# Four seven-product units in the third token tile, and the VectorE sums that have to be ready for them

## The chip, the cores and the metric

The kernel runs on one core of a Trainium2 chip. The metric is the device time of one launch in microseconds (us). The kernel before takes 278.38 us, the median of 3 runs (278.06 to 278.6). Its profiled execution took 278.12 us, of which the trace covers a span of 276.4 us; all times inside the trace are counted from the start of that span. The granted TensorE clock was 0.999 of full speed over the run.

## What is computed

Two stages, one after the other. The first is an attention over pooled keys and values, the second a gated feed-forward product over its output:

```python
# q, k, v: 8 batches, 8 heads, 576 positions, 64 values per head
k_p, v_p = k and v averaged over groups of 8 positions      # 72 pooled positions
attn = softmax(q @ k_p^T / sqrt(64))
x = (attn @ v_p), heads side by side                        # 4608 tokens x 512
h = x @ w_in                                                # 4608 x 2048
g = h * sigmoid(h)
out = g @ w_out                                             # 4608 x 512, float32
```

## The kernel before

The 4608 tokens are worked off in nine **tiles** `t = 0..8` of 512 tokens. In each tile TensorE does an "up" product (`x @ w_in`, transposed so that `h_T` has the 2048 hidden values on 16 groups `g` of 128 partitions), ScalarE applies SiLU, TensorE does a "down" product (`h @ w_out`), and in between it computes the attention of the batch that later tiles need.

Most of the large products use **seven products of quarter blocks in place of eight**. Seven products numbered 1 to 7 take sums or differences of blocks on both sides, and VectorE and ScalarE combine the results. In the up product such a **unit** covers four of the sixteen groups; the units are called A, B, C and E here and in the kernel's token strings, so `C5` is product 5 of unit C. The weight sums of a unit never change and are made once; the sums of x (`x_sum`) are made anew for each tile:

```python
    UNITS = ((4, 6), (8, 10), (12, 14), (0, 2))      # A, B, C, E: groups of two
    U_W = {2: ((1, 0), (1, 1)), 5: ((0, 0), (0, 1)), 1: ((0, 0), (1, 1)),
           6: ((1, 0), (0, 0)), 7: ((0, 1), (1, 1))}  # five weight sums for each unit
    ...
    def unit_weight_sum(y, n):                        # L442, 128x512 bf16 on VectorE
        nc.vector.tensor_tensor(out=w_sum1[y][U_WI[n]], in0=UW[y][a], in1=UW[y][b], op=...)
    def unit_x_sum(t, n):                             # L449, 128x512 bf16 on VectorE
        nc.vector.tensor_tensor(out=x_sum[:, U_XI[n]], in0=x_quarter(t, *a), in1=x_quarter(t, *b), op=...)
    def unit_x(t, n):
        if n in U_XI:
            return x_sum[:, U_XI[n]]
        return x_quarter(t, 0, 0) if n == 2 else x_quarter(t, 1, 1)   # products 2 and 5: x itself
    ...
        def stage(y, n):          # bank P takes products 2, 4, 7; Q takes 5, 3, 6; R takes 1
            if n == "2":
                product(y, 2, "P", True)
                nc.scalar.copy(r_sb, ps[y, "P"])
            elif n == "5":
                product(y, 5, "Q", True)
                tt(out=rr_sb, in0=ps[y, "Q"], in1=r_sb, op=ALU.add)       # L514
            elif n == "1":
                product(y, 1, "R", True)
                tt(out=t_sb, in0=ps[y, "R"], in1=rr_sb, op=ALU.subtract)  # L517
            elif n == "3":
                product(y, 3, "Q", False)     # adds to bank Q, so rr_sb must have been read
                hidden(y, 0, 1, ps[y, "Q"])
            ...                               # 4, 7, 6: L526, L529 and the SiLU of the results
```

One product of a unit is four matmuls of 256 columns. A group that is not in a unit is a plain product: four matmuls of 512 columns (`plain`, L547).

Three recipes exist, chosen by the tile:

- **t = 0**: plain products up and down.
- **t = 1 and 2**: `up` with an item list (two units and eight plain groups in t = 1; three units A, B, C and the plain groups 0 to 3 in t = 2), then `down_quarters`, the down product in seven products that begins with products 2 and 5. VectorE's and other work is placed by step: a list entry `(step, function)` is recorded once that many steps of TensorE's work have been recorded.
- **t = 3 to 8** (`t >= T4`): `run(t)`, one fixed token string with four units, whose down product (`down_stages`) begins with product 4, on plain h, and has its products interleaved with the up product's end.

```python
    PROGRAM = (
        "C2 C5 B2 B5 q0 C4 C1 C3 q3 B4 C7 B3 B1 Ca C6 A2 Cs B7 A5 B6 E2 A4 Ba E5 A1 Bs "
        "A3 h7h A7 E4 E3 q1 E1 A6 Aa k As E7 q2 E6 d40 d41 d42 Ea h5h d43 h2h d30 Es "
        ...
        "d52 d53 d10 sc2 de1 h6h d11 h7l u2 d12 d13 d70 nu0 nu1 de2 d71 T2 d72 d73 d60 "
        "x3 d61 d62 x7 x6 d63 o x4 x1 "
    )
```

In `run`, the tokens `u1` and `u2` are two subtractions on GpSimd (L754), behind the loads of the next batch in GpSimd's program. The part of `down_quarters` that ends a tile t = 1 or 2, with the work that is recorded among it:

```python
            product(3, 0, KQ, cc)
            nc.vector.tensor_copy(out=o_sb[0][:, cs, HI], in_=ps["Q"][:, cs])               # L682
            product(7, 0, KQ, cc)
            tt(out=o_sb[0][:, cs, LO], in0=ps["P"][:, cs], in1=t_sb[:, cs], op=add)         # L686
            ...
            product(6, 0, KQ, cc)
            tt(out=o_sb[1][:, cs, HI], in0=ps["Q"][:, cs], in1=t_sb[:, cs], op=add)         # L690
    ...
        # attention of batch a: the last part of xT that the next tile needs
        tensor_mul(out=xT[...], in0=nu[c], in1=rec)                                         # L398
        # sums of x for the next tile
            for n in (4, 1, 3, 7, 6):
                f_down.append((98 if t < B - 1 else 44, lambda n=n: unit_x_sum(t + 1, n)))
        if t == 1:
            ...
            f_down.append((72, unit_weight_tiles))
            for i, n in enumerate(U_W):
                f_down.append((73 if i < 2 else 81, lambda n=n: unit_weight_sum(2, n)))
        if t == 2:
            for i, n in enumerate(U_W):
                f_down.append((76 + 2 * i, lambda n=n: unit_weight_sum(3, n)))
```

Besides these, `hidden_sum(n, k0, k1)` (L615) makes the sums of h for the down product, half of the groups at a time (`h2` lower half, `h1` upper half and so on), and `weight_sum(n, i)` (L633) makes quarters of the down product's weight sums.

Of the kernel before, what the change touches and what calls it, by code (L numbers as in the profile page):

```python
# [36 lines left out]
def kernel(  # L37
# [11 lines left out]
    B, H, S, D = q.shape  # L49
# [90 lines left out]
    def load_q(b, halves=False):  # L140
        st = batches.setdefault(b, {})
        q_bf = mid.tile([128, 2, QI * D], BF16, tag="q_bf", name="q_bf")
        if halves:
            pass
        elif b == B - 1:

            for s in range(4):
                for a in range(2):
                    nc.gpsimd.dma_start(
                        out=q_bf[QP * s : QP * (s + 1), a, :].rearrange(  # L150
                            "p (i d) -> p i d", d=D
                        ),
                        in_=q[b, 4 * a + s].rearrange("(i p) d -> p i d", p=QP),
                    )
        else:
            nc.gpsimd.dma_start(out=q_bf, in_=q_r[b])
        st["q_bf"] = q_bf
        st["qT"] = mid.tile([128, 2, QI, QP, 2], BF16, tag="qT", bufs=1, name="qT")
# [41 lines left out]
    def behind_x_sums(n=6):  # L200
        nc.gpsimd.tensor_copy(out=gate[:1], in_=x_sum[:1, U_XI[n], 0, :1])

    def pool_k(b):
        pool_rows(kp[:SP], batches[b]["k_raw"])
# [114 lines left out]
    def part(g, f):  # L319
        return ((g, f * QF, (f + 1) * QF),)  # L320
# [3 lines left out]
    def third(n):  # L324
        return tuple((g, n * QV, (n + 1) * QV) for g in range(2))
# [31 lines left out]
    def denominators(b, segs, on_dve=False):  # L357
        st = batches[b]
        w = width(segs)
        es = st["es", segs]  # L360
        den_ps = ps_tile([128, 512], FP32, "at", "den_ps")
        for s in range(4):
            nc.tensor.matmul(  # L363
                den_ps[32 * s : 32 * (s + 1), :w],
                lhsT=ones, rhs=es[:, s, :], start=True, stop=True,
            )
        rec = mid.tile([128, VW], FP32, tag="rec", bufs=3, name="rec")[:, :w]
        if on_dve:
            nc.vector.reciprocal(rec, den_ps[:, :w])
        else:  # L370
            lnd = mid.tile([128, VW], FP32, tag="lnd", bufs=1, name="lnd")[:, :w]
            nc.scalar.activation(lnd, den_ps[:, :w], func=AF.Ln)  # L372
            nc.scalar.activation(rec, lnd, func=AF.Exp, scale=-1.0)
        st["rec", segs] = rec

    def numerators(b, segs, tags=("at", "at")):
        st = batches[b]
        w = width(segs)
        g0, i0, i1 = segs[0]
        c0 = b * S % NX + i0 * QP  # L380
        cols = slice(c0, c0 + (i1 - i0) * QP)
        es = st.pop(("es", segs))
        rec = st.pop(("rec", segs))
        nu = []
        for c in range(2):
            nu_ps = ps_tile([128, 512], FP32, tags[c], "nu_ps")
            for g, _, _, cs in seg_cols(segs):
                for s in range(4):
                    nc.tensor.matmul(  # L389
                        nu_ps[32 * s : 32 * (s + 1), cs],  # L390
                        lhsT=st["vp"][:, 4 * g + s, c::2],
                        rhs=es[:, s, cs],
                        start=True, stop=True,
                    )
            nu.append(nu_ps)
        ng = len(segs)
        for c in range(2):
            nc.vector.tensor_mul(  # L398
                out=xT[:, 2 * g0 + c : 2 * (g0 + ng - 1) + c + 1 : 2, cols],
                in0=nu[c][:, :w].rearrange("r (g n) -> r g n", g=ng),  # L400
                in1=rec.rearrange("r (g n) -> r g n", g=ng),
            )
# [8 lines left out]
    def spread(fillers, n):  # L411
# [5 lines left out]
        for f in todo:  # L417
# [11 lines left out]
    U_W = {2: ((1, 0), (1, 1)), 5: ((0, 0), (0, 1)), 1: ((0, 0), (1, 1)),  # L429
           6: ((1, 0), (0, 0)), 7: ((0, 1), (1, 1))}  # L430
# [9 lines left out]
    def unit_weight_sum(y, n):  # L440
        a, b = U_W[n]
        nc.vector.tensor_tensor(  # L442
            out=w_sum1[y][U_WI[n]], in0=UW[y][a], in1=UW[y][b],
            op=ALU.subtract if n in (6, 7) else ALU.add,
        )

    def unit_x_sum(t, n):
        a, b = U_X[n]
        nc.vector.tensor_tensor(  # L449
            out=x_sum[:, U_XI[n]], in0=x_quarter(t, *a), in1=x_quarter(t, *b),  # L450
            op=ALU.subtract if n in (3, 4) else ALU.add,
        )
# [148 lines left out]
    def quarter(i, j, ks):  # L601
        return h_T[:, j * KQ + ks.start : j * KQ + ks.stop, i * NQ : (i + 1) * NQ]
# [9 lines left out]
    def hidden_sum(n, k0, k1):  # L612
        a, b, op = H_SUMS[n]
        ks = slice(k0, k1)
        nc.vector.tensor_tensor(  # L615
            out=h_sum[n][:, ks, :], in0=quarter(*a, ks), in1=quarter(*b, ks), op=op
        )
# [10 lines left out]
    PW = 4  # L628
# [156 lines left out]
    def run(t):  # L785
# [13 lines left out]
        if a == B - 1:  # L799
            toks.insert(1 + max(toks.index("de2"), toks.index("nu1"), toks.index("o")), "nu2")  # L800
        if t == T4:
            toks.insert(0, "T2")
        if attn:
            if a + 1 < B - 1:
                load_q(a + 1)
            behind_x_sums(6 if t == T4 else gate_on)
            pool_k(a)
# [131 lines left out]
    def load_half_2(name, half):  # L939
        for i0, i1 in ((0, SA), (SA, SLOTS), (SLOTS, SLOTS + 1)):  # L940
            load_slots(nc.gpsimd, 2, name, i0, i1, half)

    THREE = (
        "A2 A5 g0 B2 A4 A1 A3 B5 C2 A7 B4 A6 Ah B1 B3 As C5 B7 C4 B6 Bh C1 C3 C7 Bs g1"
        " C6 Ch Cs g2 g3",
        "A2 A5 g0 A4 B2 A3 A1 B5 A7 C2 A6 B4 B3 B1 C5 Ah B7 As C4 Bh B6 C1 C3 C7 Bs g1"
        " C6 Ch Cs g2 g3",
    )
    visits = [third(n) for n in range(3)]
    T4 = 3  # L950
    for t in range(NT):
        a = t + 1
        if t >= T4:
            run(t)
            continue
        f_up, f_down = [], []
        if t == 0:
            GA = 11
            items = [(g, 0, HS) for g in range(GA)]
            items += [(g, HS, NTT - HS) for g in range(GA)]  # L960
            items += [(g, 0, NTT) for g in range(GA, KG)]
            f_up += [(1, lambda: denominators(0, part(0, 1), on_dve=True))]
            f_up += [(5, lambda: denominators(0, part(1, 1), on_dve=True))]
            f_up += [(13, lambda: numerators(0, part(0, 1)))]
            f_up += [(17, lambda: numerators(0, part(1, 1)))]
        else:
            G = lambda *gs: [(g, 0, NTT) for g in gs]
            if t == 1:
                items = (
                    G(12, 13, 14, 15) + [(0, "25143"), (1, "2"), (0, "7"), (1, "5")]  # L970
                    + [(0, "6h"), (1, "1")] + G(0) + [(1, "4"), (0, "s"), (1, "3")] + G(1)
                    + [(1, "7h6")] + G(2) + [(1, "s")] + G(3)
                )
            else:
                items = []
                for it in THREE[t // B].split():
                    items += [(("BCA".index(it[0])), it[1])] if it[0] in "ABC" else G(int(it[1]))
            if t == 1:
                for n in U_X:
                    f_up.append((0, lambda n=n: unit_x_sum(t, n)))  # L980
            for n in (2, 5):
                h_at = 50 if t == B else 54 if t > 1 else 45
                f_up.append((h_at, lambda n=n: hidden_sum(n, 4, 8)))
            f_up.append((56, lambda: hidden_sum(6, 4, 8)))
            for n, k0 in ((2, 0), (5, 0), (1, 4), (1, 0)):
                f_up.append((64, lambda n=n, k0=k0: hidden_sum(n, k0, k0 + 4)))
            f_down.append((33 if t > 1 else 44, lambda: hidden_sum(7, 0, 8)))
            f_down.append((71 if t < B else 50, lambda: hidden_sum(6, 0, 4)))

        for n, t0, f_to, at, parts in (  # L990
            (1, 0, f_down, 16, (0, 2)), (3, 0, f_down, 30, (0, 2)),
            (1, 0, f_down, 46, (2, PW)), (3, 0, f_down, 50, (2, PW)),
            (6, 0, f_down, 8, (0, PW)), (4, 0, f_down, 12, (0, 2)),
            (7, 0, f_down, 14, (0, 2)), (4, 1, f_down, 20, (2, PW)), (7, 1, f_down, 52, (2, PW)),
        ):
            for i in range(*parts):
                if t == t0:
                    f_to.append((at + i, lambda n=n, i=i: weight_sum(n, i)))
# [63 lines left out]
        if t == 1:  # L1062
# [6 lines left out]
            f_down.append((72, unit_weight_tiles))  # L1069
            for i, n in enumerate(U_W):  # L1070
                f_down.append((73 if i < 2 else 81, lambda n=n: unit_weight_sum(2, n)))
        if t == 2:
            for i, n in enumerate(U_W):
                f_down.append((76 + 2 * i, lambda n=n: unit_weight_sum(3, n)))
        if t != 1:
            moe_tables()
        if t == 0:
# [34 lines left out]
```

The softmax here doesn't subtract the row's maximum and nothing guards it: scores larger than these inputs give would overflow.

## Time and profile before

| | |
|---|---|
| time | 278.38 us (278.06 to 278.6) |
| span of the trace | 276.4 us |
| TensorE busy | 271.7 us, 98% |
| VectorE busy | 243.9 us, 88% |
| ScalarE busy | 192.4 us, 70% |
| GpSimd busy | 111.6 us, 40% |
| tile t = 1, down part | 64.69 to 80.88 us |
| tile t = 2 | 80.88 to 109.61 us |
| tile t = 3 | 109.61 to 137.95 us |

The tile boundaries are the starts of the first matmul of each part in the timeline of TensorE. In the timelines each row is a run of like instructions of one engine: start in us, time in us from the first's start to the last's end, engine, source line, operation, output tile and input tiles, shapes, count, and in brackets the idle time before the row and what ended it. The share of busy time is an average; to learn what a change in one tile is worth, one has to look at who waits for whom in that tile, and the start-to-start distances of the matmuls show best whether TensorE went on without a pause.

### The profile page before, as it was taken

The numbers are of one execution on the slowest core, as the hardware profiler recorded it, in microseconds if no ns is written. First come the engines' busy times: TensorE is split into PE (matmuls) and PEld (weight loads), VectorE is DVE, ScalarE is ACT, GpSimd is POOL, SyncE is SP. The second block draws the span as 40 slices with busy tenths as digits, with TensorE's granted clock in tenths as the row PEclk, the third lists the DMA queues.
The fourth block names the chain that finished last, engine by engine and source line by source line (L and its number), as shares of the span: only waits on it lengthen the run. The fifth ranks groups of instructions, "written<-read, shape, count | busy, mean of one in ns | idle before, by whom it ended". The sixth has DMA issues, their size and how long they took to land.

```text
span 276.4 us, 7372 instructions
## 1 busy us (share of the span) xinstructions
PE 271.7 (98%) x2933; PEld 209.7 (76%) x2933; DVE 243.9 (88%) x452; ACT 192.4 (70%) x374; POOL 111.6 (40%) x112
## 2 busy tenths in 40 slices
PE   8999999999999999999999999999999999999995
PEld 4448444576778678887888778877887788888884
DVE  4986778778998879998999999999999899998994
ACT  1688767468668976789777986798688868407730
POOL 8755116252148530964377426976450400000000
PEclk9999999999999999999999999999999999999999
DMA  7999999986849879468746844599620032005003
GB/s 214 276 245 252 207 306 196 257 161 118 165 56 216 228 106 180 119 180 127 129 115 176 144 72 126 135 155 128 131 66 2 2 100 55 0 12 145 1 26 129
DMA packets 31314, 37.73 MB, mean 137 GB/s; under 512 B 10352, under 2 KB 22256, under 8 KB 31280
## 3 DMA queue, kind: packets, MB, share of 16 engines
q0 software_dynamic: 23920, 27.03, 52.7%
q1 hardware_dynamic: 6928, 9.58, 12.5%
q10 hardware_dynamic: 432, 0.66, 0.6%
q8 instruction: 23, 0.38, 0.6%
q14 instruction: 11, 0.09, 0.1%
HBM read 36.70 MB, written 9.44 MB: 167 GB/s over the span
## 4 chain that ended last, share of the span: by engine, by line
PE 83%; DMA 14%; issue 1%; POOL 0%; DVE 0%; POOLq 0%
PE u_psP L493 14%; PE u_psQ L493 14%; PE o_psQ L712 12%; PE o_psP L712 12%; DMA w_in_sb<-in_moe_w_in_dram 6%; DMA w_out_sb<-in_moe_w_out_dram 6%; PE u_psR L493 5%; PE o_psR L712 4%; PE o_psQ L656 4%; PE o_psP L656 4%; PE hp_ps L547 4%; PE sc_ps L345 3%; PE nu_ps L389 3%; PE o_ps L582 2%; DMA q_bf<-in_q_dram 2%; PE den_ps L363 2%
## 5 line engine op out<-in xcount | busy, mean ns | idle before, releaser
L615 DVE TENSOR_TENSOR h_sum<-h_T 128x1024 bf16<-128x1024 bf16 (+1 forms) x78 | 59.2, 803 | 2.8 <-ACT h_T L501 1.6
L493 PEld LDWEIGHTS <-w_sum 128*128 128x128 bf16 x532 | 52.0, 98 | 7.2 <-issue 0.3
L712 PEld LDWEIGHTS <-h_sum 128*128 128x128 bf16 x480 | 45.8, 98 | 8.1 <-issue 2.5
L353 ACT ACTIVATE es<-sc_ps 72x384 bf16<-72x384 f32 (+1 forms) x100 | 39.1, 471 | 5.4 <-PE sc_ps L345 5.3
L501 ACT ACTIVATE h_T<-c_sb 128x512 bf16<-128x512 f32 x58 | 35.7, 630 | 6.2 <-DVE c_sb L529 3.6
L511 ACT COPY r_sb<-u_psP 128x512 f32<-128x512 f32 x29 | 17.0, 586 | 19.2 <-PE u_psP L493 19.2
L547 PE MATMUL hp_ps<-xT,w_in_sb 128*128 128x512 bf16 (+2 forms) x156 | 26.6, 319 | 0.0
L398 DVE TENSOR_TENSOR xT<-nu_ps,rec 128x384 bf16<-128x384 f32 (+1 forms) x50 | 23.9, 529 | 1.7 <-PE nu_ps L389 1.4
L493 PEld LDWEIGHTS <-w_in_sb 128*128 128x128 bf16 x232 | 22.5, 98 | 3.2 <-DVE x_sum L449 0.3
L195 POOL TENSOR_TENSOR raw<-raw 72x1024 f32<-72x1024 f32 x10 | 23.6, 2365 | 0.1
L514 DVE TENSOR_TENSOR rr_sb<-u_psQ,r_sb 128x512 f32<-128x512 f32 x29 | 19.5, 684 | 3.6 <-PE u_psQ L493 1.9
L559 POOL DMA_DIRECT2D out_dram<-o_sb x2 | 1.2, 617 | 52.2 <-ACT o_sb L726 48.1
L553 ACT ACTIVATE h_T<-hp_ps 128x512 bf16<-128x512 f32 (+2 forms) x39 | 18.1, 477 | 5.9 <-PE hp_ps L547 5.1
L526 DVE TENSOR_TENSOR c_sb<-u_psP,t_sb 128x512 f32<-128x512 f32 x29 | 19.8, 682 | 1.9 <-PE u_psP L493 1.3
L547 PEld LDWEIGHTS <-w_in_sb 128*128 128x128 bf16 x156 | 14.6, 98 | 8.5 <-issue 0.8
L517 DVE TENSOR_TENSOR t_sb<-u_psR,rr_sb 128x512 f32<-128x512 f32 x29 | 19.6, 676 | 1.5 <-PE u_psR L493 0.5
L754 POOL TENSOR_TENSOR rr_sb<-rr_sb,o_sb 128x512 f32<-128x512 f32 x8 | 14.3, 1782 | 15.9 <-ACT o_sb L726 12.6
L529 DVE TENSOR_TENSOR c_sb<-u_psQ,t_sb 128x512 f32<-128x512 f32 x29 | 19.6, 677 | 1.0 <-PE u_psQ L493 0.8
L712 PEld LDWEIGHTS <-h_T 128*128 128x128 bf16 x192 | 18.5, 98 | 2.7
L501 ACT ACTIVATE h_T<-u_psP 128x512 bf16<-128x512 f32 x29 | 17.3, 598 | 3.5 <-PE u_psP L493 3.5
L501 ACT ACTIVATE h_T<-u_psQ 128x512 bf16<-128x512 f32 x29 | 17.3, 596 | 3.4 <-PE u_psQ L493 3.4
L372 ACT ACTIVATE lnd<-den_ps 128x384 f32<-128x384 f32 (+1 forms) x23 | 11.2, 487 | 11.3 <-PE den_ps L363 11.3
(106 smaller groups left out, 585.4 us busy)
## 6 DMA issues: line engine op xcount, KB each, us to landing
out_dram<-o_sb SPq DMA_DIRECT2D x128, 64.0 KB, 1.8
raw<-in_k_dram POOLq DMA_DIRECT2D x10, 576.0 KB, 7.9
raw<-in_v_dram POOLq DMA_DIRECT2D x10, 576.0 KB, 7.7
q_bf<-in_q_dram POOLq DMA_DIRECT2D x6, 576.0 KB, 10.6
w_in_sb<-in_moe_w_in_dram POOLq DMA_DIRECT2D x8, 256.0 KB, 8.3
w_out_sb<-in_moe_w_out_dram POOLq DMA_DIRECT2D x4, 512.0 KB, 13.5
raw<-in_v_dram POOLq DMA_DIRECT2D x2, 768.0 KB, 11.1
raw<-in_k_dram POOLq DMA_DIRECT2D x1, 768.0 KB, 10.7
```

Source lines behind the costliest of these rows:

```text
L195: nc.gpsimd.tensor_add(out=raw[:, :, : 2 * D], in0=raw[:, :, : 2 * D], in1=raw[:, :, 2 * D :])
L353: nc.scalar.activation(es[:, s, :], sc[s], func=AF.Exp, scale=score_scale)
L398: nc.vector.tensor_mul(out=xT[:, 2 * g0 + c : 2 * (g0 + ng - 1) + c + 1 : 2, cols], in0=nu[c][:, :w].rearrange("r (g n) -> r g n", g=ng), ...
L493: nc.tensor.matmul(ps[y, bank][:, u, :], lhsT=w[:, kk, 128 * u : 128 * (u + 1)], rhs=x[:, kk, :], start=first and u == 0 and kk == 0, stop ...
L501: nc.scalar.activation(h_T[:, g : g + 2, j * NQ : (j + 1) * NQ], src, func=AF.Silu)
L517: tt(out=t_sb, in0=ps[y, "R"], in1=rr_sb, op=ALU.subtract)
L526: tt(out=c_sb[0], in0=ps[y, "P"], in1=t_sb, op=ALU.add)
L529: tt(out=c_sb[1], in0=ps[y, "Q"], in1=t_sb, op=ALU.add)
L547: nc.tensor.matmul(hp_ps[:, r0:r1], lhsT=w_in_sb[:, kk, g * 128 : (g + 1) * 128], rhs=xT[:, kk, x0 : x0 + r1 - r0], start=(kk == 0), stop= ...
L615: nc.vector.tensor_tensor(out=h_sum[n][:, ks, :], in0=quarter(*a, ks), in1=quarter(*b, ks), op=op)
L656: nc.tensor.matmul(ps[b][:, c, :], lhsT=left(n, kt, c), rhs=W_OUT[n][:, kt, :], start=b not in begun, stop=kt == k1 - 1, skip_group_check= ...
L712: nc.tensor.matmul(ps[b][:, c, :], lhsT=left(n, kt, c), rhs=W_OUT[n][:, kt, :], start=b not in begun, stop=kt == k1 - 1, skip_group_check= ...
```

## The change

The token string with four units is used from tile 2 on, no longer from tile 3. That does three things in tile 2: the four plain groups become unit E; the down product begins with product 4, on plain h, as in the tiles behind it; and two subtractions go to GpSimd. The five weight sums of unit E, which tile 2 made for tile 3, must now be ready in tile 2, so tile 1 makes them, right after the sums of unit C. To make room for them, tile 1 makes the upper half of `h1` and half of the down weight sum 4 earlier, at a place where VectorE was idle.

```diff
-    THREE = ( ... token strings of the three-unit up product ... )
     visits = [third(n) for n in range(3)]
-    T4 = 3
+    T4 = 2
     for t in range(NT):
         a = t + 1
         if t >= T4:
             run(t)
             continue
 ...
-            if t == 1:
+            if True:
                 items = ( ... tile 1, as it was ... )
-            else:
-                items = []
-                for it in THREE[t // B].split(): ...
 ...
             f_up.append((56, lambda: hidden_sum(6, 4, 8)))
-            for n, k0 in ((2, 0), (5, 0), (1, 4), (1, 0)):
+            f_up.append((57, lambda: hidden_sum(1, 4, 8)))
+            for n, k0 in ((2, 0), (5, 0), (1, 0)):
                 f_up.append((64, lambda n=n, k0=k0: hidden_sum(n, k0, k0 + 4)))
 ...
-            (7, 0, f_down, 14, (0, 2)), (4, 1, f_down, 20, (2, PW)), (7, 1, f_down, 52, (2, PW)),
+            (7, 0, f_down, 14, (0, 2)), (4, 1, f_up, 58, (2, PW)), (7, 1, f_down, 52, (2, PW)),
 ...
             for i, n in enumerate(U_W):
                 f_down.append((73 if i < 2 else 81, lambda n=n: unit_weight_sum(2, n)))
-        if t == 2:
-            for i, n in enumerate(U_W):
-                f_down.append((76 + 2 * i, lambda n=n: unit_weight_sum(3, n)))
+                f_down.append((84, lambda n=n: unit_weight_sum(3, n)))
```

More of the change, by code (lines that the diff above doesn't have):

```diff
@@ L941, in load_half_2 @@
             load_slots(nc.gpsimd, 2, name, i0, i1, half)
[L943 to L948, printed above, removed]
     visits = [third(n) for n in range(3)]
-    T4 = 3
+    T4 = 2
     for t in range(NT):
@@ L973 @@
                 )
-            else:
-                items = []
-                for it in THREE[t // B].split():
-                    items += [(("BCA".index(it[0])), it[1])] if it[0] in "ABC" else G(int(it[1]))
             if t == 1:
```

## The prediction, made before the changed kernel ran

> **What bounds the kernel now.** I read the page's first part, then the three tiles concerned as stretches, then the timelines of TensorE and VectorE at the border of tiles 1 and 2. The first part gives the shares.
>
> ```profile
> PE 271.7 (98%) x2933; PEld 209.7 (76%) x2933; DVE 243.9 (88%) x452; ACT 192.4 (70%) x374; POOL 111.6 (40%) x112
> ```
>
> TensorE is busy for 98% of the span, so what counts is the length of its queue and any pause in it. VectorE, at 88%, has little room. The stretches below are tile 1's down part, tile 2 and tile 3 (time, then busy time of PE, PEld, DVE, ACT, POOL with counts, clock, DMA share, GB/s).
>
> ```profile
> 64.69:80.88 16.19, 16.19 (x218) 12.75 (x217) 15.08 (x33) 12.07 (x25) 4.40 (x4) 1.00 0.53 96
> 80.88:109.61 28.73, 28.73 (x326) 22.64 (x324) 24.82 (x47) 22.34 (x43) 12.66 (x10) 1.00 0.93 179
> 109.61:137.95 28.34, 28.34 (x338) 23.88 (x336) 26.51 (x48) 23.30 (x44) 16.04 (x12) 1.00 0.69 139
> ```
>
> Two things are to be seen. Tile 3 already has the recipe that tile 2 is to get, with the same attention work, and is 28.73 - 28.34 = 0.39 us shorter: that is the prize. And VectorE is busy for 15.08 of 16.19 us in tile 1's down part, which is where five more of its instructions go. The timeline of VectorE shows the end of that part:
>
> ```profile
> 76.94 0.68 DVE L682 COPY o_sb<-o_psQ 128x512 f32<-128x512 f32 x1
> 77.54 1.09 DVE L442 TENSOR_TENSOR w_sum<-w_in_sb 128x512 bf16<-128x512 bf16 x3
> 78.67 0.69 DVE L686 TENSOR_TENSOR o_sb<-o_psP,t_sb 128x512 f32<-128x512 f32 x1
> 79.30 1.02 DVE L398 TENSOR_TENSOR xT<-nu_ps,rec 128x384 bf16<-128x384 f32 x2
> 80.24 1.76 DVE L449 TENSOR_TENSOR x_sum<-xT 128x512 bf16<-128x512 bf16 x5
> 81.91 0.69 DVE L690 TENSOR_TENSOR o_sb<-o_psQ,t_sb 128x512 f32<-128x512 f32 x1
> 82.51 0.68 DVE L514 TENSOR_TENSOR rr_sb<-u_psQ,r_sb 128x512 f32<-128x512 f32 x1
> ```
>
> No row has a bracket: from 76.94 on VectorE never pauses. What it does there is not spare work: the two xT rows are the last tokens of x that tile 2 reads, x_sum its summed operands, and rr_sb frees the bank that a later product adds to. TensorE's timeline gives when tile 2 asks for them; the last line is the place in tile 1 discussed further down.
>
> ```profile
> 80.88 0.60 PE L493 MATMUL u_psP<-xT,w_sum 128*128 128x256 bf16 x4
> 81.31 0.60 PE L493 MATMUL u_psQ<-xT,w_sum 128*128 128x256 bf16 x4
> ...
> 67.01 1.04 PE L656 MATMUL o_psP<-w_out_sb,h_sum 128*128 128x256 bf16 x8
> ```
>
> The second row is product 5, the first that needs the second half of the tile's tokens. They are written at 79.30 + 1.02 = 80.32, it starts at 81.31: about 0.99 us to spare.
>
> **What the Trainium skill says.** "Perfetto Trace Analysis", Identifying the Most-Contended Engine, warns that matmul busy share is no good measure of distance from the roofline. The trace agrees: the 98% is with weight loads at 76%, and a pause shows only in start-to-start distances. "TensorE: Matmul & The Clock Gate", in the opening table, lists VectorE's queue as strictly first in, first out: an instruction put ahead delays all behind it. The trace's order is the program's order everywhere I looked. "VectorE: DVE Perf Modes", The perf-mode tier table, gives tensor_tensor two bf16 results a cycle from SBUF and one with PSUM operands. The trace agrees in kind: the 512-element bf16 sums last 418 ns on average, rr_sb (fp32, PSUM) 684 ns. Sums are cheap, but not free.
>
> **The change part by part.**
>
> *Unit E in place of four plain groups.* One product of a unit is four matmuls at 0.436 us together (141.01 - 137.96 for seven products in tile 4); a plain group takes 0.86 us (82.61 - 81.75). So 7 x 0.436 - 4 x 0.86 = -0.39 to -0.40 us on TensorE, the same as the tile difference. VectorE gets four combining instructions of E (0.60 apart, +2.4 us) and loses the five weight sums. All of it lies as in tile 3, where TensorE does not pause for it.
>
> *The down product from plain h, and u1, u2.* No matmul is added or lost. In tile 3 these run without a pause of TensorE, so I give them 0.
>
> *An h sum and two weight sums earlier in tile 1.* VectorE idles from 65.12 to 66.11 (the h sum at 64.44 lasts 0.68). Into this go an h sum (0.60 from start to start) and two weight sums (0.34 each). The next h sum, `h2` lower half, starts at 64.44 + 0.60 + 0.60 + 2 x 0.34 = 66.32 in place of 66.11 and ends at 66.99; the product that reads it starts at 67.01, and its weight load must come before that. I expect a pause of about 0.1. The time won behind it on VectorE is of no use: L682 waits for TensorE's product 3 anyway.
>
> *Five weight sums of E in tile 1.* In the changed program they stand between L682 and L686, so the three sums at 77.54 become eight. One more costs 0.335 us: (1.76 - 0.42) / 4 from the x_sum row of the same shape. Five are 1.68 us, and with no pause to absorb them everything behind moves by that:
>
> - xT done at 80.32 + 1.68 = 82.00. Tile 2 now begins with C2, C5, B2, B5, C4, C1, C3. C5 wants to start at 81.31 and can at 82.05, with 0.05 for the signal: a pause of **0.74**.
> - x_sum for C4 done at 80.24 + 0.42 + 1.68 = 82.34; C4 comes at 82.05 + 3 x 0.436 = 83.36. No pause.
> - rr_sb of C done at 82.51 + 0.68 + 1.68 = 84.87. C3 adds to the bank that rr_sb reads, and would come at 82.05 + 5 x 0.436 = 84.23. It can at 84.92: another **0.69**.
> - Behind that I walked both queues on to E3. From A5 to E3 each product finds VectorE 0.5 us or more ahead of it, apart from those where VectorE itself waits for TensorE. No further pause.
>
> Together: TensorE is 0.74 + 0.69 = 1.43 us late at C3. The 0.05 and the reading of C3 come from tile 6 of the kernel before, where x sums were late (TensorE: the end of B5, then C4, C1, C3; VectorE: the last two x sums and the first two rr_sb):
>
> ```profile
> 195.95 0.60 PE L493 MATMUL u_psQ<-xT,w_sum 128*128 128x256 bf16 x4
> 196.55 0.61 PE L493 MATMUL u_psP<-x_sum,w_in_sb 128*128 128x256 bf16 x4
> 197.00 0.60 PE L493 MATMUL u_psR<-x_sum,w_sum 128*128 128x256 bf16 x4
> 197.48 0.60 PE L493 MATMUL u_psQ<-x_sum,w_in_sb 128*128 128x256 bf16 x4
> ...
> 196.08 0.75 DVE L449 TENSOR_TENSOR x_sum<-xT 128x512 bf16<-128x512 bf16 x2
> 196.75 1.28 DVE L514 TENSOR_TENSOR rr_sb<-u_psQ,r_sb 128x512 f32<-128x512 f32 x2
> ```
>
> C4 comes 0.60 behind B5 and not 0.44: the x sum ended at 196.08 + 0.42 = 196.50, C4 started at 196.55. C3 comes 0.48 behind C1: the first rr_sb ended at 196.75 + 0.68 = 197.43, C3 started at 197.48. Signals take 0.05 us, and both waits are real.
>
> The sum: 278.38 - 0.39 + 1.43 + 0.1 = 279.5 us.
>
> **Rivals.** *The pauses stay away.* If VectorE came to L682 earlier, or the sums overlapped more, only the prize would stay: 278.0 us. For it speaks the idle gap that the change fills. Against it: L682 waits for TensorE, so time won before it is lost there, and the five sums are behind it.
>
> *GpSimd becomes the wait.* Its gate for tile 2 follows the last x sum, so its loads move by 1.68 too; u1 sits behind the load that was issued at 99.80 in the kernel before and is now at about 101.5. I place u1's end at 104 to 104.6 and u2's at about 106.2; t_sb of product 1 wants it at 133.91 - 109.61 + 80.88 + 1.43 = 106.6. It fits by 0.4 us. DMA share in tile 2 is 0.93, so loads that land later could add up to 1 us here: 280 to 280.5.
>
> *VectorE recovers late in tile 2.* It has 26.5 of 28.3 us of work in such a tile. If it lagged on to the h sums, further pauses of some tenths would come: 280. Against it: tile 3 shows VectorE idle for 0.31 at 118.18 and for 1.25 at 131.02, so it catches up.
>
> **Range and chances.** The pauses follow from durations that the trace shows, so I put the centre on them. The low end is the first rival with half a microsecond of pauses, the high end the second one. 278.5 to 280.2 us holds it 8 times in 10. Two per cent are 5.6 us, which no rival reaches: faster 0.01, same 0.97, slower 0.02.
>
> **What would show it.** In the changed profile's timelines: eight L442 instructions behind L682 and L686 near 80.35; C5 about 1.2 us behind C2 in place of 0.44; C3 waiting for rr_sb, some 1.1 us behind C1; from E on, 0.436 steps without pauses; tile 2 about 29.8 us from first matmul to tile 3's first; tile 1 longer by 0.1 at most. It would be wrong if xT or rr_sb ended much earlier than 82.0 and 84.9, or if t_sb in tile 2's down part waited for GpSimd.

## The result, and the profile after

The changed kernel takes 279.17 us, the median of 6 runs (278.81 to 279.74); the kernel before takes 278.38 us (277.8 to 278.6). The ratio is 1.0034, with a 95% interval of 1.0018 to 1.005: a small loss, where the recipe with four units by itself would save 0.39 us (tile 3 against tile 2 in the profile before). The profile after is of the slowest of the six runs, 279.74 us, with a span of 278.0 us.

Its first part, and the beginning of the chain that ended last by engine; the last row is that chain before the change:

```profile
PE 271.4 (98%) x2945; PEld 210.5 (76%) x2945; DVE 247.8 (89%) x457; ACT 192.9 (69%) x375; POOL 114.2 (41%) x114
...
PE 80%; DMA 12%; DVE 4%; POOL 2%; issue 1%; DVEq 0%; POOLq 0%
...
PE 83%; DMA 14%; issue 1%; POOL 0%; DVE 0%; POOLq 0%
```

TensorE's busy time went down by 0.3 us, as intended, while the span grew: TensorE now waits. The chain tells on whom. VectorE held 0% of it before and holds 4% now: mainly 6.0 us at the border of tiles 1 and 2, and 2.9 us at that of tiles 5 and 6. GpSimd's 2% are no such sign: its pieces lie in the first 8 us of the launch, and kernel 7 below, the fastest one, has the same 2%. The stretches of tile 1's down part, tile 2 and tile 3 (time, busy time of PE, PEld, DVE, ACT and POOL with counts, clock, DMA share, GB/s):

```profile
64.93:81.11 16.18, 16.18 (x218) 12.65 (x216) 15.28 (x35) 12.06 (x25) 4.41 (x4) 1.00 0.56 99
81.11:110.65 29.54, 28.71 (x339) 23.84 (x336) 29.15 (x51) 23.36 (x44) 15.68 (x12) 1.00 0.87 165
110.65:139.00 28.35, 28.35 (x339) 23.88 (x337) 27.82 (x48) 22.65 (x43) 15.68 (x12) 1.00 0.76 148
```

Tile 1's down part is as long as before (16.18 and 16.19) and so is tile 3; tile 2 takes 29.54 where it took 28.73. In none of these three stretches did TensorE's busy time fall short of the time before; in tile 2 it now does, 28.71 of 29.54. VectorE's timeline at the border of tiles 1 and 2 (start, time, line, tiles, shapes, count):

```profile
77.10 0.69 DVE L682 COPY o_sb<-o_psQ 128x512 f32<-128x512 f32 x1 [0.19 <-PE o_psQ L656]
77.71 2.09 DVE L442 TENSOR_TENSOR w_sum<-w_in_sb 128x512 bf16<-128x512 bf16 x6
79.72 0.75 DVE L442 TENSOR_TENSOR w_sum1e<-w_in_sb 128x512 bf16<-128x512 bf16 x2
80.39 0.68 DVE L686 TENSOR_TENSOR o_sb<-o_psP,t_sb 128x512 f32<-128x512 f32 x1
80.99 1.01 DVE L398 TENSOR_TENSOR xT<-nu_ps,rec 128x384 bf16<-128x384 f32 x2
...
84.20 1.28 DVE L514 TENSOR_TENSOR rr_sb<-u_psQ,r_sb 128x512 f32<-128x512 f32 x2
```

The three weight sums have become eight, and xT ends at 80.99 + 1.01 = 82.00 although tile 2 began at 81.11. TensorE, from C2 and C5 to C1 and C3:

```profile
81.11 0.60 PE L493 MATMUL u_psP<-xT,w_sum 128*128 128x256 bf16 x4
81.59 0.27 PE L493 MATMUL u_psQ<-xT,w_sum 128*128 128x256 bf16 x1
82.06 0.49 PE L493 MATMUL u_psQ<-xT,w_sum 128*128 128x256 bf16 x3 [0.20 <-DVE xT L398]
...
83.69 0.60 PE L493 MATMUL u_psR<-x_sum,w_sum 128*128 128x256 bf16 x4
84.93 0.60 PE L493 MATMUL u_psQ<-x_sum,w_in_sb 128*128 128x256 bf16 x4 [0.64 <-DVE rr_sb L514]
```

Both waits have their bracket, and it names VectorE's xT and rr_sb. The brackets give the idle time behind the modelled end of the matmul before; the start-to-start distances give the loss. C5 is broken in two, and C3 starts 1.24 us behind C1 instead of 0.44. Without a pause C3 would start six products behind C2, at 81.11 + 6 x 0.436 = 83.73; it starts at 84.93, 1.20 us late.

### The profile page after: what moved, and what is told of

Read it like the earlier page. It is cut to its first block, busy times and chain, and to the rows that moved or that the text cites. A ratio compares the mean times of both kernels' runs of the same rounds, so it can differ in the third digit from the quotient of the medians.

```text
span 278.0 us, 7416 instructions
## 1 busy us (share of the span) xinstructions
PE 271.4 (98%) x2945; PEld 210.5 (76%) x2945; DVE 247.8 (89%) x457; ACT 192.9 (69%) x375; POOL 114.2 (41%) x114
## 4 chain that ended last, share of the span: by engine, by line
PE 80%; DMA 12%; DVE 4%; POOL 2%; issue 1%; DVEq 0%; POOLq 0%
PE u_psQ L493 14%; PE u_psP L493 13%; PE o_psP L712 13%; PE o_psQ L712 13%; DMA w_in_sb<-in_moe_w_in_dram 7%; DMA w_out_sb<-in_moe_w_out_dram 6%; PE o_psR L712 5%; PE u_psR L493 5%; PE sc_ps L345 3%; PE nu_ps L389 3%; PE hp_ps L547 2%; PE o_ps L582 2%; PE o_psP L656 2%; PE den_ps L363 2%; PE o_psQ L656 1%
## 5 line engine op out<-in xcount | busy, mean ns | idle before, releaser
L615 DVE TENSOR_TENSOR h_sum<-h_T 128x1024 bf16<-128x1024 bf16 x79 | 61.9, 827 | 1.5 <-ACT h_T L501 1.4
L712 PEld LDWEIGHTS <-h_sum 128*128 128x128 bf16 x560 | 53.4, 98 | 9.5 <-issue 3.1
L493 PEld LDWEIGHTS <-w_sum 128*128 128x128 bf16 x544 | 53.1, 98 | 7.3 <-issue 0.7
L493 PEld LDWEIGHTS <-w_in_sb 128*128 128x128 bf16 x240 | 23.3, 98 | 4.7 <-DVE x_sum L449 0.9
L754 POOL TENSOR_TENSOR rr_sb<-rr_sb,o_sb 128x512 f32<-128x512 f32 x10 | 17.2, 1723 | 16.5 <-ACT o_sb L726 11.5
L712 PEld LDWEIGHTS <-h_T 128*128 128x128 bf16 x224 | 21.5, 98 | 3.2
L547 PE MATMUL hp_ps<-xT,w_in_sb 128*128 128x512 bf16 (+2 forms) x140 | 22.7, 313 | 0.0
L553 ACT ACTIVATE h_T<-hp_ps 128x512 bf16<-128x512 f32 (+2 forms) x35 | 15.9, 464 | 5.1 <-PE hp_ps L547 4.4
L493 PE MATMUL u_psP<-x_sum,w_in_sb 128*128 128x256 bf16 x120 | 18.2, 273 | 0.6 <-DVE x_sum L449 0.6
L493 PE MATMUL u_psQ<-x_sum,w_in_sb 128*128 128x256 bf16 x120 | 18.0, 272 | 0.6 <-DVE rr_sb L514 0.6
```

What stands on the lines that cost most here:

```text
L493: nc.tensor.matmul(ps[y, bank][:, u, :], lhsT=w[:, kk, 128 * u : 128 * (u + 1)], rhs=x[:, kk, :], start=first and u == 0 and kk == 0, stop ...
L547: nc.tensor.matmul(hp_ps[:, r0:r1], lhsT=w_in_sb[:, kk, g * 128 : (g + 1) * 128], rhs=xT[:, kk, x0 : x0 + r1 - r0], start=(kk == 0), stop= ...
L615: nc.vector.tensor_tensor(out=h_sum[n][:, ks, :], in0=quarter(*a, ks), in1=quarter(*b, ks), op=op)
L712: nc.tensor.matmul(ps[b][:, c, :], lhsT=left(n, kt, c), rhs=W_OUT[n][:, kt, :], start=b not in begun, stop=kt == k1 - 1, skip_group_check= ...
```

## The experiments

**Theory 1**: the five weight sums hold up VectorE's queue, and xT and rr_sb come late. **Theory 2**: the new recipe costs the time in tile 2 by itself, through GpSimd's two subtractions or the change over from tile 1's recipe. Four kernels tell them apart. "Tile 2" and "tile 6" in the tables are read in TensorE's timeline, from the first matmul of the tile to that of the next.

**1. Without the sums.** Unit E multiplies with unit C's sums, so this kernel leaves out five instructions and its hidden values are not those of the reference.

```diff
-                w_sum1.append([v_w[:, 1 + i] for i in range(3)] + [w_e[:, i] for i in range(2)])
+                w_sum1.append(w_sum1[2])
-                f_down.append((84, lambda n=n: unit_weight_sum(3, n)))
```

> The changed kernel without the five weight sums of unit E: E multiplies with unit C's sums, so its hidden values are not the reference's; all else is as in the changed kernel. Theory 1 (the five sums hold up the VectorE queue at the end of tile 1): C5 follows C2 by 0.44 us, C3 follows C1 by 0.44, tile 2 takes 28.35 us as tile 3 does, and the time is 0.4 us under the kernel before: 278.0 us. Theory 2 (tile 2's new recipe itself costs the time: GpSimd's two subtractions, or the change over from tile 1's recipe): tile 2 stays at 29.5 us and the time at 279.2 us.

**2. The sums alone.** The kernel before, three units in tile 2, with the sums of E made in tile 1.

```diff
                 f_down.append((73 if i < 2 else 81, lambda n=n: unit_weight_sum(2, n)))
-        if t == 2:
-            for i, n in enumerate(U_W):
-                f_down.append((76 + 2 * i, lambda n=n: unit_weight_sum(3, n)))
+                f_down.append((84, lambda n=n: unit_weight_sum(3, n)))
```

> The kernel before, with three units in tile 2, but the five weight sums of unit E are made in tile 1, where the changed kernel makes them. Theory 1: A5 pauses for xT by about 0.4 us, and A3, which there has a plain group's 0.86 us more before it, follows when rr_sb is read, 0.77 us late in all; tile 2 takes 28.73 + 0.77 = 29.5 us, and the time is 279.15 us. Theory 2: the time of the kernel before, 278.4 us.

**3. Three more of them.**

```diff
                 f_down.append((84, lambda n=n: unit_weight_sum(3, n)))
+            for n in (2, 5, 1):
+                f_down.append((84, lambda n=n: unit_weight_sum(3, n)))
```

> The changed kernel with three of the five weight sums of unit E made twice, at the same place. Theory 1: three more instructions at 0.335 us, all on the path: C3 another 1.0 us later, tile 2 takes 30.55 us, and the time is 1.0 us over the changed kernel: 280.2 us. Theory 2: no more than the changed kernel, 279.2 us.

**4. The same sums, earlier.** E takes the buffers that are free early in tile 1, C takes the others.

```diff
-                k_w = big.tile([128, 4, 2, 256], BF16, tag="k_raw2", name="w_sum12")
                 v_w = big.tile([128, 4, 2, 256], BF16, tag="v_raw2", name="w_sum12")
-                w_sum1.append([k_w[:, i] for i in range(4)] + [v_w[:, 0]])
-                w_sum1.append([v_w[:, 1 + i] for i in range(3)] + [w_e[:, i] for i in range(2)])
+                w_sum1[2] = [v_w[:, i] for i in range(4)] + [w_e[:, 0]]
+            def unit_e_tiles():
+                k_w = big.tile([128, 4, 2, 256], BF16, tag="k_raw2", name="w_sum12")
+                w_sum1.append(None)
+                w_sum1.append([k_w[:, i] for i in range(4)] + [w_e[:, 1]])
+            f_up.append((1, unit_e_tiles))
+            for n in U_W:
+                f_up.append((1, lambda n=n: unit_weight_sum(3, n)))
-                f_down.append((84, lambda n=n: unit_weight_sum(3, n)))
```

> The changed kernel with the five weight sums of unit E made early in tile 1's up part, before the first rr_sb, where VectorE was idle for 1.74 us; their buffers are swapped with unit C's so that this is possible. Output as the reference. Theory 1: 5 x 0.335 = 1.68 us fit the gap, tile 1 grows by 0.1 at most, tile 2 takes 28.35 us, and the time is 278.0 us, under both kernels. Theory 2: tile 2 at 29.5 us, 279.2 us.

| kernel | time, us | ratio to before (95%) | tile 2 | tile 6 |
|---|---|---|---|---|
| before, beside 1 to 4 | 278.1 | 1 | 28.73 | 29.10 |
| changed | 279.17 (before: 278.38) | 1.0034 (1.0018 to 1.005) | 29.54 | 29.68 |
| 1 without the sums | 278.03 | 0.9994 (0.9979 to 1.0008) | 28.34 | 29.40 |
| 2 the sums alone | 278.9 | 1.0031 (1.0016 to 1.0045) | 29.57 | 29.24 |
| 3 three more | 279.83 | 1.0071 (1.0048 to 1.0093) | 30.55 | 29.03 |
| 4 the sums earlier | 278.01 | 0.9998 (0.9985 to 1.0011) | 28.34 | 29.55 |

Tile 2 does what theory 1 says in all four. Without the sums it is 28.34 us, as tile 3; with five 29.54; with eight 30.55, so one more sum costs (30.55 - 29.54) / 3 = 0.34 us, its whole start-to-start distance. The sums alone cost 0.84 us in tile 2 of a kernel that has nothing of the new recipe. Theory 2 falls. TensorE's timeline with three more sums has the same two waits, the first of them longer:

```profile
81.88 0.27 PE L493 MATMUL u_psQ<-xT,w_sum 128*128 128x256 bf16 x1 [0.89 <-DVE xT L398]
82.34 0.49 PE L493 MATMUL u_psQ<-xT,w_sum 128*128 128x256 bf16 x3 [0.20 <-DVE xT L398]
...
85.21 0.49 PE L493 MATMUL u_psQ<-x_sum,w_in_sb 128*128 128x256 bf16 x3 [0.64 <-DVE rr_sb L514]
```

With the sums earlier, VectorE's timeline shows where they went and what became of L686:

```profile
53.82 1.43 DVE L442 TENSOR_TENSOR w_sum<-w_in_sb 128x512 bf16<-128x512 bf16 x4
55.16 0.42 DVE L442 TENSOR_TENSOR w_sum1e<-w_in_sb 128x512 bf16<-128x512 bf16 x1
55.53 0.69 DVE L514 TENSOR_TENSOR rr_sb<-u_psQ,r_sb 128x512 f32<-128x512 f32 x1
...
77.85 0.42 DVE L442 TENSOR_TENSOR w_sum1e<-w_in_sb 128x512 bf16<-128x512 bf16 x1
78.38 0.69 DVE L686 TENSOR_TENSOR o_sb<-o_psP,t_sb 128x512 f32<-128x512 f32 x1
```

They end at 55.58, and the first rr_sb starts on time, 4.76 us after tile 1's first matmul as before: five instructions, and tile 1 is no longer (29.80 us; before 29.81). Yet kernels 1 and 4, with 0.39 us less in tile 2, don't show it in their times: they lie within 0.1 us of the kernel before, and kernel 4's interval, 0.9985 to 1.0011, holds both no gain and the expected one. The last column suggests where it went. From tile 1 on, all tiles but 2 and 6 agree to 0.02 us in the six profiles; tile 6 varies by 0.65 us. (Tile 1's first matmul, behind the first loads, also varies, from 50.58 to 51.30 us; why is open.) Each kernel has one profile, so this alone does not tell chance from an effect of the kernels' differences.

**5 to 7. What lengthens tile 6.** Tile 5 loads the last batch, whose q comes in eight pieces on GpSimd's queue. GpSimd's timeline in the kernel before, the eighth piece and then the two subtractions:

```profile
183.88 0.66 POOL L149 DMA_DIRECT2D q_bf<-in_q_dram  x1 [1.37 <-DMA raw<-in_v_dram]
...
186.33 4.61 POOL L754 TENSOR_TENSOR rr_sb<-rr_sb,o_sb 128x512 f32<-128x512 f32 x2
```

The same rows of the changed kernel:

```profile
185.92 0.67 POOL L149 DMA_DIRECT2D q_bf<-in_q_dram  x1 [2.35 <-DMA raw<-in_v_dram]
...
188.38 4.62 POOL L754 TENSOR_TENSOR rr_sb<-rr_sb,o_sb 128x512 f32<-128x512 f32 x2
```

The eighth piece waits for the v load before it, and the subtractions stand behind. Counted from tile 5's first matmul (166.30 and 167.34) it starts at 17.58 before and 18.58 after, and VectorE after, whose t_sb needs the subtractions, shows the wait:

```profile
189.36 2.50 DVE L615 TENSOR_TENSOR h_sum<-h_T 128x1024 bf16<-128x1024 bf16 x2
193.03 0.69 DVE L735 TENSOR_TENSOR t_sb<-o_psR,rr_sb 128x512 f32<-128x512 f32 x1 [1.17 <-POOL rr_sb L754]
```

Before, t_sb has no such bracket, nor has it in the other four profiles. There the subtractions start earlier in the tile, beside more of the h sums, and the h sums themselves take longer (more on this in the last section). VectorE's timeline before:

```profile
184.22 3.93 DVE L615 TENSOR_TENSOR h_sum<-h_T 128x1024 bf16<-128x1024 bf16 x4
188.67 2.83 DVE L615 TENSOR_TENSOR h_sum<-h_T 128x1024 bf16<-128x1024 bf16 x2
191.42 0.68 DVE L735 TENSOR_TENSOR t_sb<-o_psR,rr_sb 128x512 f32<-128x512 f32 x1
```

Either way t_sb comes late: 25.12 us after tile 5's first matmul before, 25.69 after. From there VectorE goes on without a pause to the x sums of tile 6, and C4 waits for them. It started 0.60 us behind B5 before (shown in the prediction) and starts 1.18 behind it now:

```profile
196.99 0.60 PE L493 MATMUL u_psQ<-xT,w_sum 128*128 128x256 bf16 x4
198.17 0.61 PE L493 MATMUL u_psP<-x_sum,w_in_sb 128*128 128x256 bf16 x4 [0.57 <-DVE x_sum L449]
```

Over the six profiles the eighth piece starts at 17.52, 17.58, 17.72, 17.88, 18.04 and 18.58 us, and tile 6 takes 29.03, 29.10, 29.24, 29.40, 29.55 and 29.68, in the same order of kernels (three more, before, the sums alone, without, earlier, changed). To test it, tile 5's two subtractions go to VectorE, in the kernel before, the changed one and number 4:

```diff
-                (nc.gpsimd if t < B - 1 else nc.vector).tensor_tensor(
+                (nc.gpsimd if t < B - 1 and t != B - 3 else nc.vector).tensor_tensor(
```

> The kernel before, with the two subtractions on rr_sb (u1, u2) of tile 5 alone put on VectorE, where they can't wait behind GpSimd's loads. Question: where the differences in tile 6's length come from (29.0 to 29.7 us in the six profiles so far, longer the later the v rows of batch 7 land in tile 5). If GpSimd's queue is the cause, tile 6 takes 28.8 to 28.9 us, product 1's t_sb starts at most 24.0 us after tile 5's first matmul, and the time is 278.1 - 0.3 = 277.8 us with less spread. If it is something else, tile 6 stays between 29.0 and 29.7.

> The changed kernel with the same alteration in tile 5. With GpSimd's wait out of the way, the change's own effect should stand alone: tile 6 as in before_u5, tile 2 at 29.54 us, 0.81 us over that kernel: 278.6 us. If the change had a second effect on tile 6, its tile 6 would be longer than that of before_u5.

> The version with unit E's weight sums in tile 1's idle gap, with the same alteration in tile 5. Tile 2 at 28.34 us, 0.39 us under before_u5; tile 6 as there; the time 277.4 us, and 0.7 us under the kernel before (ratio 0.9975), if the 0.39 us of the four-unit recipe were hidden by tile 6's spread only. If the early sums cost something that the profile doesn't show, no less than before_u5.

| tile 5's subtractions on VectorE | time, us | ratio to before (95%) | tile 2 | tile 6 |
|---|---|---|---|---|
| 5 before, altered (unaltered beside it: 278.14) | 277.86 | 0.9987 (0.9978 to 0.9996) | 28.73 | 28.88 |
| 6 changed | 278.5 | 1.0013 (1.0006 to 1.0021) | 29.54 | 28.88 |
| 7 the sums earlier | 277.42 | 0.9981 (0.9972 to 0.999) | 28.34 | 28.88 |

Tile 6 takes 28.88 us in all three, and t_sb (kernel 5: 190.30 - 166.29) starts 24.01 us after tile 5's first matmul. So the spread came through the two subtractions on GpSimd, as a wait of t_sb or as longer h sums. That the landing of v sets its size rests on the order of the six profiles alone, and whether v lands later by chance or through the change is open. With the spread gone the rest adds up: the changed recipe costs 278.5 - 277.86 = 0.64 us (0.81 in the profiles), and with the sums in the gap it saves 277.86 - 277.42 = 0.44 us (0.39 in the profiles). The intervals of 5 and 6 lie apart. Those of 5 and 7 overlap, but 12 of the 22 runs of kernel 7 are faster than the fastest of the 14 of kernel 5 (277.5). Kernel 7 is the fastest of all, 0.7 us under the kernel before. It owes that to two alterations: five sums in a gap in which VectorE was idle, and two subtractions taken off a queue that waits for loads.

## Why the prediction was right

**The mechanism held, step by step.** Five sums in front of L686, C5 waiting for xT, C3 for rr_sb, no pause behind C3: all are in the timelines above, and experiments 1 to 4 tie them to the sums. The prize was right to 0.01 us (28.73 - 28.34).

**The terms.** Predicted were -0.39 + 1.43 + 0.1; tile 2 shows -0.39 + 1.20, tile 1 nothing. Two terms were too large, and the first of them was split wrongly.

- *"with no pause to absorb them everything behind moves by that"*, 1.68 us. From C2 on, xT ended at 80.32 - 80.88 = -0.56 before and ends at 82.00 - 81.11 = +0.89 now: it moved by 1.45. The missing 0.23 were waits for TensorE in the kernel before that had no bracket. L682 starts 4.01 us ahead of C2 now and 3.94 before, so there 0.07 was won by the earlier h sum, which the prediction held to be of no use. L686 shows the next one: it starts 2.20 us ahead of C2 in kernel 4 (78.38 to 80.58) and 2.21 before (78.67 to 80.88), though kernel 4's sums end earlier against C2 (78.27, 2.31 ahead, against 78.63, 2.25 ahead). So it waited for product 7 (whose modelled end is 78.28 there and 78.58 before, 0.1 us ahead of it in both), not for the sums. Rows without a bracket were read as a queue without pause; gaps of 0.1 us don't get one.
- *The split into 0.74 and 0.69* came out as 0.40 and 0.80, since C5's first matmul needs only the first of the two xT instructions, and the three behind it wait for the second. For the sum this is of no account: rr_sb ends when VectorE's queue says, and C3's start is set by that alone, whatever C5 has lost before.
- *The pause of 0.1 in tile 1*: tile 1 takes 29.81 us before and after. The product in question starts 0.90 behind the one before it in place of 0.87, and the 0.03 are regained.

Part of the agreement is luck. xT and rr_sb end at 82.00 and 84.88, as predicted to 0.01 us, but in this profile tile 2 begins 0.23 us later than before (81.11 and 80.88), which just hides the 0.23 us by which the delay was put too high.

**The rivals.** The pauses did not stay away, and VectorE did not lag further: tile 2 is 28.34 + 1.20 = 29.54 us, so behind C3 nothing more is lost. GpSimd did not become the wait in tile 2. There u2 ends at 106.40 (the prediction said about 106.2), and t_sb starts at 106.87 without a bracket:

```profile
104.82 1.58 POOL L754 TENSOR_TENSOR rr_sb<-rr_sb,o_sb 128x512 f32<-128x512 f32 x1 [1.29 <-DVE o_sb L731]
106.87 0.68 DVE L735 TENSOR_TENSOR t_sb<-o_psR,rr_sb 128x512 f32<-128x512 f32 x1
```

The same subtractions do cost time in tile 5, in the kernel before as well, which the prediction did not consider. Of the 1.6 us between the two profiled spans they make 0.58 (29.68 - 29.10); 0.81 are tile 2, and 0.24 the start (tile 1's first matmul at 51.30 and 51.06). Whether any of the 0.58 belongs to the change is open. By the times it can be little on average: the changed kernel is 0.79 us over the kernel before, and 0.64 with tile 5's subtractions moved in both. The predicted time of 279.5 is 0.3 over the measured one, which is what the two terms were too large by (0.23 and 0.1).

## What to carry to other kernels

An instruction that fits an engine's share of busy time may still stand in front of the one that the next stage begins with. So ask of a place in an in-order queue what comes behind it and when that is wanted, and look for a place whose next customer is already waiting for something else: here the same five sums cost 1.2 us of TensorE's time in one gap and nothing in another. When several waits follow from one late queue, count to the last of them, not their sum. And before a small gain is judged by total times, find the stage whose length differs between profiles for another reason: 0.39 us did not show in the times until tile 6 stood still.

## What the runs showed of the hardware that was not expected

VectorE's h sums slow down while GpSimd's subtractions run. While L754 runs on GpSimd (186.33 to 190.94 before, 188.38 to 193.00 after), the last two in tile 5 take 2.83 us before and 2.50 after, as shown above. The four ahead of them take 3.93 us before, and 2.48 in the changed kernel, where they are over by 187.74, ahead of L754. With the subtractions on VectorE (kernel 5, its timeline) the last two take half as long:

```profile
188.31 1.28 DVE L615 TENSOR_TENSOR h_sum<-h_T 128x1024 bf16<-128x1024 bf16 x2
189.51 0.68 DVE L754 TENSOR_TENSOR rr_sb<-rr_sb,o_sb 128x512 f32<-128x512 f32 x1
190.30 0.69 DVE L735 TENSOR_TENSOR t_sb<-o_psR,rr_sb 128x512 f32<-128x512 f32 x1
```

The subtraction itself takes 0.68 us on VectorE and on average 4.62 / 2 = 2.3 on GpSimd. So both cost VectorE 2 x 0.68 = 1.36 us, and against the kernel before these two h sums alone gave back 2.83 - 1.28 = 1.55. This agrees with the Trainium skill, "SBUF — State Buffer", section SBUF: two separate sides, which says that a VectorE instruction with two SBUF inputs and a GpSimd instruction that reads SBUF exclude each other on a shared pair of ports for a whole instruction; that the ports are the cause was not tested here.
